# RWKV-6 attention with a mixture-of-depths layer: the scores' products in quarter tiles behind the state's products, and the accumulator banks dealt out anew

## The chip, the core and the metric

The kernel runs on one core of one Trainium2 chip. The metric is the device time of one execution in microseconds. Of the kernel before there are three runs, with a median of 201.39 us (200.97 to 201.78), and one more execution that was profiled.

## What is computed

Per batch (4), head (8) and position (768), with heads of 48 elements, a state of 48 x 48 is carried through the sequence. `w` decays it, `k` and `v` add to it, `r` reads it, and the position's own product is weighted with `u`:

```python
for t in range(S):
    cur = einsum('bhd,bhe->bhde', u * k[t], v[t])
    y[t] = einsum('bhd,bhde->bhe', r[t], state + cur)
    state = w[t][..., None] * state + einsum('bhd,bhe->bhde', k[t], v[t])
x = y, as (batch, position, 384)
scores = x @ w_gate                       # per batch and position
top = the 128 positions with the highest scores
out = x;  out[top] += sigmoid(scores[top]) * (relu(x[top] @ w1) @ w2)
```

## The kernel before

**Tiling.** The sequence of a batch is cut into 6 chunks of 128 positions, 24 chunks in all. Inside a chunk the recurrence is written as matrix products. Two heads lie side by side in each 128-partition tile, 64 partitions apiece (48 used, the rest padding), so the 8 heads are 4 pairs (`HP`), and `half(q)` names the partitions of head `q` of a pair.

**What happens to a chunk.** `inputs_t` transposes k and r on the Tensor engine (PE), `decays_t` the decays w. On the Vector engine (DVE) `scans` turns the decays into running products from the right and from the left, and `scaled` multiplies the transposed k and r with them and thereby empties their accumulator banks. `scores` multiplies K with R, 128 x 128 per head; `masked` keeps what lies before the diagonal, on DVE. `outputs_t` adds up two products in one tile `ps_yt`: the masked scores with v, and, from a batch's second chunk on, the state with R. The Scalar engine (ACT) copies that to `yt`. `rows_out` transposes it back, ACT copies it to `x`, the GpSimd engine (POOL) adds the positions' own part `vo`, and the rows are stored. `own_products`, `own_weights` (POOL), `own_values` (ACT, one small sum per head) and `own_results` make that part. `back` transposes K back (`kt`, copied by ACT), `carry_products` multiplies it with v, and `carry` adds the state and multiplies by the chunk's whole decay. There is no `back`, `carry_products` or `carry` for the last chunk of a batch, and no state in the first.

**Router.** `row_products` and `row_sums` give a score per position. `compared` ranks a chunk's scores against those of its batch: it spreads a chunk's 128 scores over a bank with a transpose (`ps_e`), DVE compares that with the chunk's own (L534) and with the earlier chunks' (L530), and ACT copies it to `every` for the later chunks. When a batch is complete, `mixture` counts the ranks (products into `ps_r`, L554), builds a selection matrix (`pick`, L571), finds the chosen rows' indices (`ps_i`), gathers the rows with an indirect DMA and transposes them (`ps_x`). `forward` is the feed-forward on them, in small pieces (`ps_h` L638, `ps_f` L650).

**Order.** All engines' programs are in the order in which `turn(i)` calls these steps: `manual_schedule` moves nothing. A turn mixes chunks: it works on chunk `i`, prepares `i+1` and `i+2`, writes out `i-1` and compares `i-2`. `fed_in_turn` puts pieces of the feed-forward of an earlier batch into two places of a turn (the first and the second feed half), and `mix` moves `mixture` on by a step in named places ("half", "mid", "end"). Semaphores between engines follow from the tiles: an instruction waits for the one that wrote what it reads, and for the last reader of a buffer that it overwrites; two engines that read one accumulator bank are also put one after the other, in the program's order.

**Accumulator banks.** [...] Before, they are dealt out in pools: `psW` one (decays, and the router's `ps_e`), `psT` two in rotation (transposes of k, of r, of K back), `psS` one tile of two banks (the scores and, after them, `ps_yt`), `psY` one (rows back), `psK` one (carry products), `psM` one (feed-forward).

**Loads.** SyncE (SP) issues the loads in `loads(i + 5)` at the end of a turn, and the stores; each of r, k, v, w has four buffers.

## Time and profile before

| | |
|---|---|
| median of three runs | 201.39 us (200.97 to 201.78) |
| profiled execution | 201.83 us, of it 200.0 us from the first to the last instruction |
| PE busy (matmuls; weight loads) | 187.9 us (153.5 us) |
| DVE, ACT, POOL busy | 159.7, 127.4, 139.0 us |
| scores (L395) | 384 instructions, 27.9 us |
| products with the state (L436) | 320 instructions, 13.1 us |
| moved by DMA | 28.81 MB |
| granted clock of PE, mean | 0.982 |

PE's busy time counts matmuls that overlap, and their ends are modelled; for the time that a group really takes, the starts of one group and the next are compared. A single-precision product is two matmul instructions in the trace, a transpose is one. "Waits" name who waited for whom; idle time of an engine that isn't the bottleneck costs nothing. In a window, a DMA share near 1 means that the core's 16 DMA engines were busy throughout. Line numbers (L395) are those of the kernel before.

### The profile page before, as it was taken

The page shows a single profiled execution, that of the slowest core. Times are in us where ns is not written, and L with a number is a line of the kernel's source. Part 1 is how long each engine was busy: PE and PEld are TensorE (multiplying, and loading weights), DVE is VectorE, ACT ScalarE, POOL GpSimd, SP SyncE. Part 2 cuts the span into 40 slices and gives each one's busy share as a digit, 9 for nine tenths or more (in the row PEclk, how much of TensorE's full clock was granted, in tenths as well). Part 3 has the DMA queues.
Part 4 walks back from the last instruction along what each step waited for, and adds up shares of the span by engine and source line. Part 5 has one row for each costly group of instructions (what it writes and reads, how often), then busy time and mean ns, then how long its engine had stood idle before and what let it go on. Part 6 is the DMA issues. An engine that isn't in the chain of part 4 may idle for free.

```text
span 200.0 us, 6426 instructions
## 1 busy us (share of the span) xinstructions
PE 187.9 (94%) x2289; PEld 153.5 (77%) x2289; DVE 159.7 (80%) x348; ACT 127.4 (64%) x653; POOL 139.0 (70%) x186
## 2 busy tenths in 40 slices
PE   7999999998899999999999999999999998899980
PEld 3578878866878888897887898897787897766940
DVE  5999999999999878989978988989978984861010
ACT  4589999998955957777557667776656576410300
POOL 8699899996878797858639798857739786121202
PEclk9999999999996999999999999999999999999996
DMA  7999999998899999999995894996744121111101
GB/s 111 163 163 158 180 187 193 219 201 154 195 201 265 182 204 220 237 195 212 188 182 123 147 212 100 141 158 139 159 67 118 47 74 44 39 43 43 39 8 44
DMA packets 105387, 28.81 MB, mean 144 GB/s; under 512 B 100482, under 2 KB 104580, under 8 KB 105348
## 3 DMA queue, kind: packets, MB, share of 16 engines
q1 hardware_dynamic: 104304, 26.65, 74.8%
q0 software_dynamic: 512, 1.57, 2.6%
q8 instruction: 20, 0.33, 0.7%
q14 instruction: 19, 0.16, 0.3%
q10 hardware_dynamic: 532, 0.10, 0.3%
HBM read 22.81 MB, written 5.51 MB: 142 GB/s over the span
## 4 chain that ended last, share of the span: by engine, by line
PE 75%; ACT 8%; DVE 7%; DMA 4%; POOL 2%; issue 2%; POOLq 0%; DVEq 0%
PE ps_h L638 11%; PE ps_s L395 11%; PE ps_f L650 11%; PE ps_yt L428 8%; PE ps_t L272 7%; PE ps_kv L483 5%; PE ps_w L272 5%; PE ps_yt L436 4%; PE ps_y L279 4%; DMA r_buf<-in_r_dram 4%; PE ps_t L279 3%; PE ps_e L528 3%; ACT rk L373 2%; DVE right_buf L292 2%; ACT yt L441 2%
## 5 line engine op out<-in xcount | busy, mean ns | idle before, releaser
L373 ACT ACTIVATE rk<-rk 128x48 f32<-128x48 f32 x192 | 44.3, 238 | 0.0
L373 ACT ACTIVATION_READ_ACCUMULATOR rk<-rk 128x1 f32 x192 | 37.3, 194 | 0.0
L453 POOL TENSOR_TENSOR x<-x,vo 128x384 f32<-128x384 f32 x22 | 22.1, 1004 | 19.0 <-ACT x L452 18.9
L303 DVE TENSOR_TENSOR_SCAN left<-ps_w,from_left 128x511 f32<-128x511 f32 x24 | 30.7, 1281 | 0.9
L403 DVE TENSOR_TENSOR sc<-ps_s,before_f 128x1024 f32<-128x1024 f32 x24 | 29.2, 1218 | 2.7 <-PE ps_s L395 2.7
L395 PE MATMUL ps_s<-R,K 48*128 48x128 f32 x384 | 27.9, 285 | 2.4 <-ACT yt L441 1.6
L292 DVE TENSOR_TENSOR_SCAN right_buf<-ps_w,from_right 128x511 f32<-128x511 f32 x24 | 29.1, 1212 | 1.0 <-PE ps_w L272 1.0
L395 PEld LDWEIGHTS ps_s<-R,K 48*128 48x128 f32 x384 | 23.3, 187 | 6.6 <-ACT yt L441 4.2
L441 ACT COPY yt<-ps_yt 128x512 f32<-128x512 f32 x24 | 14.1, 586 | 19.7 <-PE ps_yt L436 18.0
L638 PE MATMUL ps_h<-xeT,w 128*128 128x128 f32 x192 | 25.6, 280 | 0.8 <-ACT hid L643 0.8
L428 PE MATMUL ps_yt<-sc,v_buf 128*64 128x128 f32 x384 | 25.6, 275 | 0.2 <-PE ps_w L272 0.2
L638 PEld LDWEIGHTS ps_h<-xeT,w 128*128 128x128 f32 x192 | 22.9, 192 | 2.9 <-issue 1.3
L362 POOL TENSOR_TENSOR rk<-r_buf,k_buf 128x384 f32<-128x384 f32 x24 | 24.1, 1002 | 0.9 <-ACT yt L441 0.9
L365 POOL TENSOR_TENSOR rk<-rk,u_bc 128x384 f32<-128x384 f32 x24 | 24.0, 1001 | 0.9 <-DVE right_buf L292 0.4
L650 PE MATMUL ps_f<-w,hid 128*128 128x384 f32 x64 | 23.8, 500 | 0.0
L458 POOL TENSOR_TENSOR scr<-x,wg_bc 128x384 f32<-128x384 f32 x22 | 22.0, 1000 | 1.7
L428 PEld LDWEIGHTS ps_yt<-sc,v_buf 128*64 128x64 f32 x384 | 20.7, 138 | 1.0 <-PE ps_w L272 0.4
L382 POOL TENSOR_TENSOR vo<-v_buf,own 128x384 f32<-128x384 f32 (+1 forms) x24 | 17.6, 735 | 3.6 <-ACT rk L373 3.6
L350 DVE TENSOR_TENSOR R<-ps_t,left 128x512 f32<-128x512 f32 x24 | 16.4, 685 | 3.3 <-ACT own L616 1.3
L539 ACT COPY every<-ps_e 128x128 f32<-128x128 f32 x20 | 5.3, 265 | 21.0 <-DVE ahead L534 21.0
L350 DVE TENSOR_TENSOR K<-ps_t,right_buf 128x512 f32<-128x512 f32 x22 | 15.0, 680 | 3.3 <-PE ps_t L272 3.3
L272 PE MATMUL ps_w<-ident,w_buf 128*128 128x128 f32 x96 | 15.6, 288 | 0.5 <-ACT every L539 0.2
(118 smaller groups left out, 368.2 us busy)
## 6 DMA issues: line engine op xcount, KB each, us to landing
k_buf<-in_k_dram SPq DMA_DIRECT2D x24, 192.0 KB, 5.3
r_buf<-in_r_dram SPq DMA_DIRECT2D x24, 192.0 KB, 5.3
v_buf<-in_v_dram SPq DMA_DIRECT2D x24, 192.0 KB, 4.5
out_dram<-x SPq DMA_DIRECT2D x24, 192.0 KB, 3.3
w_buf<-in_w_dram SPq DMA_DIRECT2D x23, 192.0 KB, 4.8
w<-in_moe_w_dram SPq DMA_DIRECT2D x3, 512.0 KB, 5.8
w<-in_moe_w_dram SPq DMA_DIRECT2D x4, 384.0 KB, 5.1
w_buf<-in_w_dram ACTq DMA_DIRECT2D x1, 96.0 KB, 3.3
```

The lines of the kernel that those rows point to most:

```text
L272: nc.tensor.transpose(ps[:, j, :], src(j), ident)
L292: nc.vector.tensor_tensor_scan(out=flat[:, W - 2::-1], data0=wt[:, W - 1:0:-1], data1=from_right.rearrange("p j t -> p (j t)")[:, W - 2::- ...
L303: nc.vector.tensor_tensor_scan(out=left.rearrange("p j t -> p (j t)")[:, 1:W], data0=wt[:, 0:W - 1], data1=start.rearrange("p j t -> p (j ...
L350: nc.vector.tensor_mul(out, t.pop(name + "t"), t.pop(by))
L362: nc.gpsimd.tensor_mul(rk, r_bufs[n % NBUF][:, :, 0:D], k_bufs[n % NBUF][:, :, 0:D])
L365: nc.gpsimd.tensor_mul(t["rk"], t["rk"], u_bc)
L373: nc.scalar.activation(out=rk[:, h, :], in_=rk[:, h, :], func=AF.Copy, accum_out=o[:, h:h + 1])
L395: nc.tensor.matmul(ps[:, q, j, :], t["K"][rows, j, :], t["R"][rows, j, :], start=True, stop=True,)
L403: nc.vector.tensor_mul(t["sc"].rearrange("p q j t -> p (q j) t"), ps.rearrange("p q j t -> p (q j) t"), _heads(before_f, 2 * HP),)
L428: nc.tensor.matmul(ps[half(c), j % 2, j // 2, :], vt[:, 2 * j + q, :], t["sc"][:, q, j, :], start=(j < 2), stop=(old is None), skip_group_ ...
L638: nc.tensor.matmul(ps[:, q, :], w1[:, dc, (f0 + q) * L:(f0 + q + 1) * L], xeT[:, dc, :], start=(dc == 0), stop=(dc == NDC - 1),)
L650: nc.tensor.matmul(ps, hid[:, fc, :], w2[:, fc, :], start=(fc == 0), stop=(fc == NFC - 1))
```

## The change

- `scores` is done in 64 x 64 tiles: for each pair, four products of 64 columns of K instead of two of 128. It is called for chunk `i+1` directly behind `outputs_t(i)`, not for chunk `i` at the start of its turn.
- `ps_yt` gets a pool of its own, `psV` (two banks); `psS` holds the scores alone. `psY` and `psK` are gone: rows back and carry products use the two rotating banks of `psT`, and the router's and feed-forward's tiles that were there, and `ps_x`, move to `psV` or `psT`.
- k of chunk `i+2` is transposed ahead of the carry products and outputs, not at the end of the turn. Its load goes one chunk further ahead, as the last of a turn's loads.
- `compared` is split in three: the earlier chunks' comparison stays, the transpose with ACT's copy (`in_all`) comes behind `back`, and the own comparison behind `masked`.

```diff
--- before.py
+++ after.py
@@ -105,8 +105,7 @@
     psW = ctx.enter_context(tc.tile_pool(name="psW", bufs=1, space=PSUM))
     psT = ctx.enter_context(tc.tile_pool(name="psT", bufs=2, space=PSUM))
     psS = ctx.enter_context(tc.tile_pool(name="psS", bufs=1, space=PSUM))
-    psY = ctx.enter_context(tc.tile_pool(name="psY", bufs=1, space=PSUM))
-    psK = ctx.enter_context(tc.tile_pool(name="psK", bufs=1, space=PSUM))
+    psV = ctx.enter_context(tc.tile_pool(name="psV", bufs=1, space=PSUM))
     psM = ctx.enter_context(tc.tile_pool(name="psM", bufs=1, space=PSUM))
 
     chunks = [(b, ci) for b in range(B) for ci in range(NCH)]
@@ -156,14 +155,14 @@
 
     def loads(n):
         load(v_bufs, v, n - 3)
-        load(k_bufs, k, n - 1)
         load(r_bufs, r, n - 1)
         load(w_bufs, w, n)
+        load(k_bufs, k, n)
 
 
     for bufs, x, n in (
         (k_bufs, k, 0), (r_bufs, r, 0), (w_bufs, w, 1), (k_bufs, k, 1), (r_bufs, r, 1),
-        (w_bufs, w, 2),
+        (w_bufs, w, 2), (k_bufs, k, 2),
     ):
         load(bufs, x, n)
     loads(3)
@@ -388,14 +387,16 @@
             )
 
     def scores(t):
+
+
         t["ps_s"] = ps = psS.tile([L, 2, HP, L], FP32, tag="s", name="ps_s")
         for j in range(HP):
-            for q in (0, 1):
-                rows = slice(DP * q, DP * q + D)
-                nc.tensor.matmul(
-                    ps[:, q, j, :], t["K"][rows, j, :], t["R"][rows, j, :],
-                    start=True, stop=True,
-                )
+            for c in (0, 1):
+                for q in (0, 1):
+                    nc.tensor.matmul(
+                        ps[half(c), q, j, :], t["K"][half(q), j, half(c)],
+                        t["R"][half(q), j, :], start=True, stop=True,
+                    )
 
     def masked(t):
         ps = t.pop("ps_s")
@@ -420,7 +421,7 @@
         vt = v_bufs[n % NBUF]
         old = state.get(n)
 
-        ps = psS.tile([L, 2, HP, L], FP32, tag="s", name="ps_yt")
+        ps = psV.tile([L, 2, HP, L], FP32, tag="v", name="ps_yt")
 
         for j in range(HP):
             for c in (0, 1):
@@ -442,7 +443,7 @@
 
     def rows_out(t, soon=False):
         b, ci = chunks[t["n"]]
-        y = dense(psY, "y", lambda j: t["yt"][0:DE, j % 2, j // 2, :], lambda j: crossed(j, 0))
+        y = dense(psT, "t", lambda j: t["yt"][0:DE, j % 2, j // 2, :], lambda j: crossed(j, 0))
         x = t["x"] = lev.tile([L, C], FP32, tag="x", name="x", bufs=3)
         xj = x.rearrange("p (j e) -> p j e", j=HP)
         vo = t.pop("vo").rearrange("p (j q) d -> p j (q d)", q=2)
@@ -477,7 +478,7 @@
         n = t["n"]
         if chunks[n][1] == NCH - 1:
             return
-        t["kv"] = kv = psK.tile([L, HP, D], FP32, tag="kv", name="ps_kv")
+        t["kv"] = kv = psT.tile([L, HP, D], FP32, tag="t", name="ps_kv")
         for j in range(HP):
             for q in (0, 1):
                 nc.tensor.matmul(
@@ -509,7 +510,7 @@
 
     against = {}
 
-    def compared(t):
+    def others_compared(t):
 
         b, ci = chunks[t["n"]]
         if ci == 0:
@@ -521,22 +522,34 @@
                 lost_bufs[b % 2],
             )
         every, ahead, lost = against[b]
-        own = score[:, b, ci:ci + 1]
-        lo, hi = ci * L, (ci + 1) * L
-
-        ps = psW.tile([L, L], FP32, tag="w", name="ps_e")
-        nc.tensor.transpose(ps, own.to_broadcast([L, L]), ident)
         if ci > 0:
             nc.vector.tensor_scalar(
-                out=ahead[:, ci, 0:lo], in0=every[:, 0:lo], scalar1=own, scalar2=None,
+                out=ahead[:, ci, 0:ci * L], in0=every[:, 0:ci * L],
+                scalar1=score[:, b, ci:ci + 1], scalar2=None,
                 op0=ALU.is_ge, op1=ALU.add, accum_out=lost[:, ci, 0:1],
             )
+
+    def in_all(t):
+
+        b, ci = chunks[t["n"]]
+        t["e"] = ps = psW.tile([L, L], FP32, tag="w", name="ps_e")
+        nc.tensor.transpose(ps, score[:, b, ci:ci + 1].to_broadcast([L, L]), ident)
+        if ci < NCH - 1:
+            nc.scalar.copy(out=against[b][0][:, ci * L:(ci + 1) * L], in_=ps)
+
+    def own_compared(t):
+        b, ci = chunks[t["n"]]
+        ahead, lost = against[b][1:]
         nc.vector.scalar_tensor_tensor(
-            out=ahead[:, ci, lo:hi], in0=ps, scalar=own, in1=after_f,
+            out=ahead[:, ci, ci * L:(ci + 1) * L], in0=t.pop("e"),
+            scalar=score[:, b, ci:ci + 1], in1=after_f,
             op0=ALU.is_ge, op1=ALU.mult, accum_out=lost[:, ci, 1:2],
         )
-        if ci < NCH - 1:
-            nc.scalar.copy(out=every[:, lo:hi], in_=ps)
+
+    def compared(t):
+        others_compared(t)
+        in_all(t)
+        own_compared(t)
 
     def mixture(b):
 
@@ -547,8 +560,11 @@
 
 
         every, ahead, lost = against[b]
-        pool, tag = (psK, "kv") if ended else (psY, "y")
-        ps = pool.tile([L, NCH], FP32, tag=tag, name="ps_r")
+        def room(shape, name):
+            pool, tag = (psT, "t") if ended else (psV, "v")
+            return pool.tile(shape, FP32, tag=tag, name=name)
+
+        ps = room([L, NCH], "ps_r")
         for e in range(NCH):
             for c in range(e + 1):
                 nc.tensor.matmul(
@@ -573,7 +589,7 @@
                     op0=ALU.is_equal,
                 )
             yield "half"
-            ps = psK.tile([L, 2], FP32, tag="kv", name="ps_i")
+            ps = room([L, 2], "ps_i")
             for c in range(NCH):
                 nc.tensor.matmul(
                     ps, pick[:, c, :], ids[:, b, c, :], start=(c == 0), stop=(c == NCH - 1)
@@ -597,7 +613,7 @@
             yield "end"
             yield "mid"
 
-            ps = psT.tile([L, NDC, L], FP32, tag="t", name="ps_x")
+            ps = room([L, NDC, L], "ps_x")
             for dc in range(NDC):
                 nc.tensor.transpose(ps[:, dc, :], xe[:, dc * L:(dc + 1) * L], ident)
             xeT = mod.tile([L, NDC, L], FP32, name="xeT", bufs=2)
@@ -631,7 +647,7 @@
         hid = mod.tile([L, NFC, L], FP32, name="hid")
         for f0 in range(0, NFC, 4):
 
-            pool, tag = (psY, "y") if ended and f0 % 8 == 0 else (psM, "m")
+            pool, tag = (psV, "v") if ended and f0 % 8 == 0 else (psM, "m")
             ps = pool.tile([L, 4, L], FP32, tag=tag, name="ps_h")
             for q in range(4):
                 for dc in range(NDC):
@@ -644,7 +660,7 @@
                 yield q == 3
 
         load_weights(len(weights))
-        pool, tag = (psY, "y") if b == B - 1 else (psM, "m")
+        pool, tag = (psV, "v") if b == B - 1 else (psM, "m")
         ps = pool.tile([L, C], FP32, tag=tag, name="ps_f")
         for fc in range(NFC):
             nc.tensor.matmul(
@@ -716,7 +732,6 @@
         if i < 1:
             step(scaled_aside, i + 1, "K", "right")
         step(own_products, i + 1)
-        step(scores, i)
         step(own_values, i, range(FIRST))
         step(carry, i - 1, work.get(i))
         if i > 0:
@@ -728,11 +743,15 @@
         if i == N - 1:
             sums.extend(check_sums())
         if i < N:
-            step(compared, i - 2)
+            step(others_compared, i - 2)
         step(back, i)
         mix(place="half")
+        if i < N:
+            step(in_all, i - 2)
         if not soon:
             step(masked, i)
+        if i < N:
+            step(own_compared, i - 2)
         step(rows_out, i - 1, soon)
         step(row_scores_soon if soon else row_products, i - 1)
         step(own_values, i, range(FIRST, H))
@@ -750,14 +769,15 @@
         if i == -1:
             spread(u_bc.rearrange("p h d -> p (h d)"), u_row)
             step(own_weights, i + 1)
+        step(inputs_t, i + 2, "K", k_bufs)
+        if i == -2:
+            warm(1)
         step(carry_products, i)
         step(outputs_t, i)
+        step(scores, i + 1)
         fed_in_turn(PIECES - PIECES // 2, 1 if i == N - 1 else 0)
         if i == N - 1:
             step(compared, i - 1)
-        step(inputs_t, i + 2, "K", k_bufs)
-        if i == -2:
-            warm(1)
         if not soon:
             step(row_sums, i - 1)
         step(scans, i + 2)
```

## The prediction, made before the changed kernel was run

> I write "turn" for one pass of the loop over chunks, and give the groups of the Tensor engine (PE) the names of their outputs: R and K (transposes of r and k), w (of the decays), kv, yt with its two halves L428 and L436 (the latter the products with the state), scores, e (the transposed scores of the router), kt and y (the back transposes). Group times are from start to start.
>
> **What bounds the kernel now.** First the page's busy line, then the table by stretches of 10 us (columns: stretch, length, busy us and instructions of each engine, granted clock, DMA share, GB/s):
>
> ```profile
> PE 187.9 (94%) x2289; PEld 153.5 (77%) x2289; DVE 159.7 (80%) x348; ACT 127.4 (64%) x653; POOL 139.0 (70%) x186
> ```
>
> ```profile
> 30.00:40.00 10.00, 9.77 (x153) 8.17 (x150) 9.79 (x20) 9.81 (x53) 9.63 (x13) 1.00 1.02 206
> 120.00:130.00 10.00, 10.00 (x142) 8.66 (x140) 9.23 (x20) 7.49 (x39) 8.58 (x11) 1.00 0.71 121
> ```
>
> Two stages: up to about 60 us VectorE (DVE), ScalarE (ACT) and the DMA engines are all full, and a turn takes 5.84 us, which is DVE's work; from 60 to 165 us PE has no gap at all, because pieces of the feed-forward fill it. Then the late PE stream in order of time (start, busy, instruction):
>
> ```profile
> 84.09 0.65 PE L436 MATMUL ps_yt<-R,state 64*48 64x128 f32 x16
> 84.67 1.60 PE L638 MATMUL ps_h<-xeT,w 128*128 128x128 f32 x12
> 86.11 0.60 PE L272 MATMUL ps_t<-ident,k_buf 128*128 128x128 f32 x4
> 86.64 1.16 PE L395 MATMUL ps_s<-R,K 48*128 48x128 f32 x16
> 87.73 0.32 PE L528 MATMUL ps_e<-ident,score 128*128 128x128 f32 x1
> ...
> 89.35 0.60 PE L272 MATMUL ps_t<-ident,r_buf 128*128 128x128 f32 x4
> 89.78 0.60 PE L272 MATMUL ps_w<-ident,w_buf 128*128 128x128 f32 x4
> 90.31 0.67 PE L483 MATMUL ps_kv<-v_buf,kt 128*64 128x48 f32 x16
> 90.81 1.06 PE L428 MATMUL ps_yt<-sc,v_buf 128*64 128x128 f32 x16
> ```
>
> Four transposes take 0.44 before more transposes (R) and 0.53 before another tile form (w, K): leaving a form costs 0.09. Entering one costs too: after L436, 12 pieces of L638 take 1.44 against 12 x 0.112 = 1.34, so 0.10.
>
> The waits (who for whom: us in all, times, longest):
>
> ```profile
> ACT every L539 <- DVE ahead L534: 21.0, 18, 2.5
> ...
> PEld ps_s L395 <- ACT yt L441: 4.2, 8, 1.1
> ```
>
> The second is what the change removes. The first shows that ACT's copy of e waits for DVE's comparison, though both only read the bank. At 40.28 that copy starts, and w, which is next in the same single bank, starts at 40.60. So bank W is a chain: e, its two readers one after the other, then w. The ACT stream of an early turn:
>
> ```profile
> 31.82 0.59 ACT L441 COPY yt<-ps_yt 128x512 f32<-128x512 f32 x1
> ...
> 34.31 0.27 ACT L539 COPY every<-ps_e 128x128 f32<-128x128 f32 x1 [0.17 <-DVE ahead L534]
> 34.47 0.49 ACT L413 COPY kt<-ps_t 128x384 f32<-128x384 f32 x1
> ```
>
> From yt to the moment ACT is ready for e is 34.31 - 0.17 - 31.82 = 2.32: a row sum, a small copy and five own-value sums.
>
> **The Trainium skill.** "TensorEngine Tiling (Array Packing)", Key Properties: changing the tiling mode drains TensorE, tiles of one mode run independently. The trace agrees: 0.09 to leave, up to 0.10 to refill. "PSUM — Partial Sum Buffer", PSUM bank collisions: two engines must not touch one bank and quadrant at once, reads included, so a dependency is put between them; the 21.0 us above are that. "TensorE: Matmul & The Clock Gate", Architectural detail: ACT and DVE are strict FIFO; the ACT stream above, in the order of the program, agrees.
>
> **The change, part by part.** *Scores.* L436 already runs in 64x64 tiles: its starts come in rounds of four, the first after 0.146, then every 0.109. The old scores start in pairs 0.112 apart, 8 rounds. The new ones are 32 instructions, thus 8 rounds of four: 8 x 0.109 + 0.09 exit = 0.96, against 1.09. The dearest they could be is the old pace per instruction, 32 x 0.068 = 2.18; the cheapest is 0.87. I take 0.96, since L436 shows the same four tiles. Form changes per turn fall from five to three. One late turn, old: w 0.53, L436 0.58, K 0.53, scores 1.09, e 0.16 = 2.89, plus the 0.09 to refill L638. New: w 0.44, K 0.53, L436 0.49, scores 0.96, e 0.11 = 2.53, plus 0.09. Saved: **0.36** per turn where PE alone sets the pace; 0.24 in the first turn of a batch, which has no L436.
>
> *Own banks for yt.* The wait of scores for ACT's yt goes (4.2). Early it hides behind DVE, so worth nothing; at 167 us, where PE really stood still 0.71, worth at most that.
>
> *Compare split.* Now DVE's masked product (1.14 to 1.22) comes ahead of the own comparison, and ACT's copy of e ahead of that too. Nothing is added to any engine, but the chain of bank W is turned round: own-values on ACT, **kt copy**, copy of e, own comparison, then w on PE; K now stands **behind w and ahead of kv and yt**, and yt feeds ACT again. Queued behind w are K, kv, yt, L436 and scores; behind the comparison on DVE are R's scaling and both scans. Sum of this loop: e copy 0.27 + release 0.06 (an ACT yt ending at 167.57 lets scores go at 167.62) + comparison 0.35 + 0.06 + w 0.44 + K 0.53 + kv 0.50 + yt 0.99 + L436 to ACT's yt 0.72 (84.09 to 84.81) + 2.32 + kt copy 0.37 = **6.61**. Before: 0.32 + w 0.53 + 0.50 + 0.99 + 0.72 + 2.32 = 5.38, under DVE's 5.84 and so unseen.
>
> Early turns (w starts at 17.40, 23.24, 29.08, 34.92, 40.60, 46.71, 52.78, 61.10, 67.82): three of 5.84 become 6.61, +2.3; into turn 5 (last chunk, no kt) 6.24 against 5.68, +0.6; the two after it lack kv or L436, +0.1 together; turn 8 has the first ranking, +0.6 (below); turn 9, 6.61 against 6.72, -0.1. With 0.3 at the start: **+3.8**.
>
> Late turns: the same loop is hidden when feed pieces lie between. Two exceptions per batch, twice:
> - Ranking. The products for it stay behind the second feed, which now stands behind scores, and the next turn begins with kt in a rotating bank that DVE must first free.
>
> ```profile
> 100.57 0.14 DVE L560 TENSOR_REDUCE rank<-lost 128x6 f32<-128x18 f32 x1
> 101.99 0.17 DVE L561 TENSOR_TENSOR rank<-ps_r,rank 128x6 f32<-128x6 f32 x1 [1.27 <-PE ps_r L554]
> 102.19 1.07 DVE L571 TENSOR_SCALAR pick<-slots,rank 128x128 bf16<-128x128 bf16 x6
> 103.17 0.35 DVE L502 TENSOR_TENSOR mid<-ps_kv,state 128x192 f32<-128x192 f32 x1
> 103.44 0.68 DVE L350 TENSOR_TENSOR K<-ps_t,right_buf 128x512 f32<-128x512 f32 x1
> ```
>
>   From rank to mid's end is 1.5, to K's end 2.1: PE, which had scores to do here, now waits that long before kt. From w to w: K, kv, yt, L436, scores, feed and ranking products end 5.9 after w, mid 7.5, then kt, index, e, y, feed, and the index and masked product on DVE hold the comparison until 9.7; w at 10.1 to 10.6, against 8.39. I take +1.8.
> - The hidden layer's activation (L643, 0.50 of ACT) at the end of a second feed half: it is ready 0.3 after the feed, then row sum, own-values 1.8, e copy, comparison 0.74: w 7.95 after w, against 6.66: +1.3.
>
> The other late turns: -0.36 -0.24 for two per batch, and about +0.15 for those whose turn has no first feed half, or a gate's sums on ACT ahead of the copy of e (both eat the 0.36). Per batch 1.8 + 1.3 - 0.6 + 0.15 = 2.65; twice, **+5.3**.
>
> *Loads.* One more load of k ahead, behind w's on SP's queue. Early, DMA is full; k landed 1.5 before its use (41.59 and 43.09) and is now wanted some 2 earlier, but issued a turn earlier: nothing. The first v comes one issue (1.15) later, for PE at 13.2: the 0.3 above. *Tail:* scores of the last chunk no longer wait, but R's scaling before them sits behind the comparison: -0.4. Ranking, index and gather banks change names only.
>
> Sum: 3.8 + 5.3 - 0.4 = +8.7. The profiled execution took 201.83 (span 200.0), 0.44 over the median of the runs, 201.39. 201.83 + 8.7 = 210.5, less 0.44: **210.1 us**, slower. I give 210.
>
> **Rivals.**
> - *Faster, PE stays the bound (0.13).* For: PE has no gap for 100 us and loses two form changes per turn. 13 turns x 0.36 + 0.71 = 5.4: 196.0. It decides if the loop of 6.61 is in truth under the turn, that is if ACT reaches the copy of e 1.2 us sooner than its queue says. Against: every link is an order of the program or a wait in this trace.
> - *Early loop only (0.13).* The late stalls are swallowed: 201.4 + 3.8 - 12 x 0.36 - 0.4 = 200.5. Against: PE can't make up lost time in a stage that it bounds.
> - *64x64 scores at the old pace (0.06).* Row pairs not overlapping: +1.2 in some 12 late turns on top, 224. Against: L436.
> - *Main (0.68):* its own range 205 to 214.
>
> Less than 0.5% either way (200.4 to 202.4) this kernel's measurement can't tell. Faster: 0.13 + 0.05 of the second rival = 0.18; same 0.05; slower 0.77. Range 199 to 215 holds the main case and the second rival, some 0.80.
>
> **What would show it.** Right: early turns of 6.6 with ACT waiting for yt and DVE's comparison waiting for ACT's copy; w waiting for the comparison; PE gaps of about 1.5 before kt at each ranking; new scores at 0.96 straight behind L436. Wrong: early turns of 5.8, PE without gaps late, or score instructions over 0.03 us each.

## The result, and the profile after

The changed kernel takes **213.13 us** (median of four runs, 212.76 to 214.19), the kernel before 201.34 beside it (200.97 to 201.78): a ratio of **1.059**, interval 1.055 to 1.064. Its profiled execution took 212.76, with a span of 211.0, so 10.9 more than the span before (spans to the hundredth: 210.97 and 200.04). One of the four executions of e1_compare_whole and one of e2_own_sums_later below, in both the profiled one, ran at a lower granted clock (0.972 and 0.971) and is left out of their medians and ratios, and those of their turns that hold a halved clock (14 in both, 20 in the first) are not compared. In this part line numbers are those of the changed kernel: scores L396, the two halves of yt L429 and L437, ACT's copy of yt L442, of e L538, of kt L414; DVE's comparison with the earlier chunks L526, the own one L543.

The page's busy line and, from its costliest groups, the scores (instructions, then busy us and mean ns):

```profile
PE 186.7 (88%) x2673; PEld 151.8 (72%) x2673; DVE 160.3 (76%) x348; ACT 128.4 (61%) x653; POOL 139.5 (66%) x186
...
L396 PE MATMUL ps_s<-R,K 64*64 64x128 f32 x768 | 26.4, 271 | 0.0
```

The engines' work has hardly changed: PE 1.2 less, DVE 0.6 more, ACT 1.0 more. Nearly all of the 11 us is standing still. The same stretches of 10 us as before show where (stretch, length, then busy us and instructions of PE, PEld, DVE, ACT, POOL, then granted clock, DMA share, GB/s); the last row will be wanted below:

```profile
30.00:40.00 10.00, 8.24 (x136) 6.84 (x136) 9.02 (x18) 9.10 (x52) 7.92 (x10) 1.00 1.21 221
120.00:130.00 10.00, 9.67 (x134) 8.37 (x133) 7.58 (x16) 7.24 (x38) 7.67 (x9) 1.00 0.63 123
110.00:115.00 5.00, 4.91 (x31) 4.04 (x32) 3.33 (x8) 2.42 (x11) 4.57 (x6) 0.66 0.20 59
```

Early, every engine lost its full occupation: PE 9.77 to 8.24, DVE 9.79 to 9.02. When all of them have slack at once, the bound is no engine, it is a ring of waits. DMA is no bound here either, although its share rose from 1.02 to 1.21: between 25 and 58 us the trace shows no engine waiting for a load. The view of waits (us in all, times, longest) has its links:

```profile
ACT yt L442 <- PE ps_yt L437: 35.2, 20, 3.7
...
PEld ps_t L271 <- ACT kt L414: 7.3, 10, 1.1
DVE ahead L543 <- ACT every L538: 6.7, 11, 1.4
PEld ps_w L271 <- DVE ahead L543: 5.6, 9, 1.1
...
PEld ps_t L278 <- DVE mid L503: 3.6, 3, 1.7
```

ACT waits for yt; PE for ACT's copy of kt and for DVE's comparison; DVE for ACT's copy of e. (The last row, mid, belongs to the ranking below.) Both rows of before that carried its story are gone, scores waiting for ACT's yt and ACT's copy of e waiting for DVE. One turn of the ring, in order of time (start, busy, instruction, idle before it):

```profile
35.08 0.59 ACT L442 COPY yt<-ps_yt 128x512 f32<-128x512 f32 x1 [0.91 <-PE ps_yt L437]
37.30 0.47 ACT L414 COPY kt<-ps_t 128x384 f32<-128x384 f32 x1
37.66 0.27 ACT L538 COPY every<-ps_e 128x128 f32<-128x128 f32 x1
37.82 0.66 PE L271 MATMUL ps_t<-ident,r_buf 128*128 128x128 f32 x4 [0.88 <-ACT kt L414]
37.96 0.35 DVE L543 SCALAR_TENSOR_TENSOR ahead<-ps_e,score,after_f 128x128 bf16<-128x128 f32 x1
38.38 0.66 PE L271 MATMUL ps_w<-ident,w_buf 128*128 128x128 f32 x4
...
40.89 0.65 PE L437 MATMUL ps_yt<-R,state 64*48 64x128 f32 x16
41.37 1.05 PE L396 MATMUL ps_s<-R,K 64*64 64x128 f32 x32
41.61 0.59 ACT L442 COPY yt<-ps_yt 128x512 f32<-128x512 f32 x1 [0.90 <-PE ps_yt L437]
```

Start to start: yt copy to kt copy 2.22, to the copy of e 0.36, to the comparison 0.30, to w 0.42, from w to K 0.49, to kv 0.53, to yt 0.50, to L437 0.99, to the next yt copy 0.72: together 6.53, which is the turn. The scores stand straight behind L437 (0.47 after its start). Two links of the same length go from ACT back to PE here: R waits 0.88 for the copy of kt, and w, which follows 0.56 behind R, has just had its comparison finished (37.96 + 0.35 = 38.31). So two links tie here, and the ring closes through either.

Two kinds of late turn stall. A ranking turn:

```profile
107.80 0.67 PE L570 MATMUL ps_r<-minus,ahead 128*128 128x1 bf16 x21
108.50 0.16 DVE L577 TENSOR_TENSOR rank<-ps_r,rank 128x6 f32<-128x6 f32 x1 [2.18 <-PE ps_r L570]
...
110.09 0.60 PE L278 MATMUL ps_t<-turned,K 112*128 112x112 f32 x4 [1.62 <-DVE mid L503]
```

DVE waits 2.18 for ranking products that stand behind a feed half, and PE then waits 1.62 for the bank that DVE empties behind the ranking. Before, the feed half stood ahead of the ranking products too, but the scores stood behind them, so that PE had work while DVE ranked:

```profile
101.28 0.67 PE L554 MATMUL ps_r<-minus,ahead 128*128 128x1 bf16 x21
101.88 1.16 PE L395 MATMUL ps_s<-R,K 48*128 48x128 f32 x16
```

And a hidden-layer turn:

```profile
85.43 0.60 ACT L659 ACTIVATE hid<-ps_h 128x512 f32<-128x512 f32 x1 [1.12 <-PE ps_h L654]
...
86.56 0.61 DVE L526 TENSOR_SCALAR_CACHE_REDUCE ahead<-every,score 128x384 bf16<-128x384 f32 x1 [1.33 <-ACT scr L464]
86.58 0.32 PE L536 MATMUL ps_e<-ident,score 128*128 128x128 f32 x1 [1.19 <-ACT scr L464]
88.64 0.66 PE L271 MATMUL ps_w<-ident,w_buf 128*128 128x128 f32 x4 [0.23 <-DVE ahead L543]
```

The activation waits for the feed, the row sum (L464, 85.92) stands behind it on ACT, and both PE (e) and DVE (the comparison with the earlier chunks) wait for the row sum.

Where the 10.9 are, from the starts of w in the two traces, turn n being the time from the start of w in turn n-1 to that in turn n:

| turns | predicted | before | after | difference |
|---|---|---|---|---|
| up to 1 | +0.3 | 17.40 | 18.22 | +0.8 |
| 2, 3, 4 | +2.3 | 5.84, 5.84, 5.84 | 7.09, 6.53, 6.53 | +2.6 |
| 5 | +0.6 | 5.68 | 6.45 | +0.8 |
| 6, 7 | +0.1 | 6.11, 6.07 | 6.34, 6.48 | +0.6 |
| 8, 9 | +0.5 | 8.32, 6.73 | 8.14, 6.54 | -0.4 |
| 11, 17 (hidden layer) | +2.6 | 6.66, 6.66 | 8.16, 8.16 | +3.0 |
| 14, 20 (ranking) | +3.6 | 8.39, 8.39 | 11.21, 10.08 | +4.5 |
| 12, 13, 18, 19 | -1.2 | 7.25, 7.06, 7.25, 7.06 | 6.95, 6.87, 6.95, 6.87 | -1.0 |
| 10, 15, 16, 21 | +0.3 | 8.04, 6.99, 8.05, 6.99 | 8.16, 7.31, 8.58, 7.05 | +1.0 |
| behind turn 21 | -0.4 | 43.41 | 42.32 | -1.1 |

### The profile page after: what moved, and what is told of

Its sections match the earlier page's. It is cut to its first block, busy times and chain, and to the rows that moved or that the text cites. A ratio compares the mean times of both kernels' runs of the same rounds, so it can differ in the third digit from the quotient of the medians.

```text
span 211.0 us, 7151 instructions
## 1 busy us (share of the span) xinstructions
PE 186.7 (88%) x2673; PEld 151.8 (72%) x2673; DVE 160.3 (76%) x348; ACT 128.4 (61%) x653; POOL 139.5 (66%) x186
## 4 chain that ended last, share of the span: by engine, by line
PE 63%; ACT 13%; DVE 11%; SPq 6%; DMA 3%; issue 3%; POOL 0%; POOLq 0%; ACTq 0%; DVEq 0%
PE ps_f L666 11%; PE ps_yt L429 9%; PE ps_h L654 7%; PE ps_t L271 7%; PE ps_yt L437 6%; PE ps_w L271 6%; PE ps_kv L484 5%; SPq L151 5%; PE ps_s L396 5%; ACT rk L372 4%; DVE sc L404 3%; PE ps_t L278 3%; DMA v_buf<-in_v_dram 3%; ACT scr L464 3%; ACT yt L442 2%
## 5 line engine op out<-in xcount | busy, mean ns | idle before, releaser
L442 ACT COPY yt<-ps_yt 128x512 f32<-128x512 f32 x24 | 14.1, 588 | 38.9 <-PE ps_yt L437 35.2
L291 DVE TENSOR_TENSOR_SCAN right_buf<-ps_w,from_right 128x511 f32<-128x511 f32 x24 | 29.2, 1216 | 2.3 <-PE ps_w L271 1.0
L396 PE MATMUL ps_s<-R,K 64*64 64x128 f32 x768 | 26.4, 271 | 0.0
L429 PE MATMUL ps_yt<-sc,v_buf 128*64 128x128 f32 x384 | 25.6, 275 | 0.0
L666 PE MATMUL ps_f<-w,hid 128*128 128x384 f32 x64 | 24.5, 511 | 0.0
L396 PEld LDWEIGHTS ps_s<-R,K 64*64 64x64 f32 x768 | 22.2, 133 | 1.3 <-issue 1.0
L429 PEld LDWEIGHTS ps_yt<-sc,v_buf 128*64 128x64 f32 x384 | 20.6, 137 | 0.6 <-issue 0.5
L271 PE MATMUL ps_t<-ident,r_buf 128*128 128x128 f32 x96 | 15.5, 285 | 5.2 <-ACT kt L414 4.6
L271 PE MATMUL ps_w<-ident,w_buf 128*128 128x128 f32 x96 | 16.2, 294 | 3.7 <-DVE ahead L543 3.4
L271 PEld LDWEIGHTS ps_t<-ident,r_buf 128*128 128x128 f32 x96 | 11.2, 145 | 9.2 <-ACT kt L414 6.7
```

The lines of the kernel that those rows point to most:

```text
L271: nc.tensor.transpose(ps[:, j, :], src(j), ident)
L291: nc.vector.tensor_tensor_scan(out=flat[:, W - 2::-1], data0=wt[:, W - 1:0:-1], data1=from_right.rearrange("p j t -> p (j t)")[:, W - 2::- ...
L396: nc.tensor.matmul(ps[half(c), q, j, :], t["K"][half(q), j, half(c)], t["R"][half(q), j, :], start=True, stop=True,)
L429: nc.tensor.matmul(ps[half(c), j % 2, j // 2, :], vt[:, 2 * j + q, :], t["sc"][:, q, j, :], start=(j < 2), stop=(old is None), skip_group_ ...
L666: nc.tensor.matmul(ps, hid[:, fc, :], w2[:, fc, :], start=(fc == 0), stop=(fc == NFC - 1))
```

## The experiments

All but one start from the changed kernel. The ratios are to the kernel before (201.2 to 201.5 in these comparisons). Single turns are from one profile each, and a stretch of halved clock can lengthen a late one by more than 1 us (last section).

| run | median, us | ratio, interval | turn 3 | 11 | 14, 20 |
|---|---|---|---|---|---|
| changed kernel | 213.13 | 1.059 (1.055 to 1.064) | 6.53 | 8.16 | 11.21, 10.08 |
| e1_compare_whole | 211.36 | 1.047 (1.041 to 1.054) | 6.60 | 7.84 | 10.29, 10.76 |
| e2_own_sums_later | 210.27 | 1.047 (1.042 to 1.052) | 6.27 | 8.15 | 11.46, 10.09 |
| e3_k_at_end | 220.21 | 1.096 (1.090 to 1.102) | 6.64 | 7.72 | 10.10, 10.11 |
| e4_feed_behind_ranking | 208.68 | 1.038 (1.034 to 1.042) | 6.53 | 7.35 | 8.70, 8.71 |
| e5_old_tiles | 214.54 | 1.068 (1.063 to 1.074) | 6.52 | 8.37 | 11.68, 10.30 |
| e6_before_new_tiles | 200.92 | 0.998 (0.996 to 1.000) | 5.78 | 6.61 | 8.39, 8.39 |
| e7_sums_and_feed | 205.00 | 1.020 (1.015 to 1.025) | 6.27 | 6.80 | 8.71, 8.71 |
| e10_whole_sums_feed | 207.09 | 1.027 (1.022 to 1.032) | 6.32 | 6.99 | 8.39, 8.39 |
| e13_copy_behind_kt | 203.99 | 1.014 (1.010 to 1.018) | 6.32 | 6.94 | 8.39, 8.39 |
| e14_and_v_first | 204.16 | 1.013 (1.009 to 1.018) | 6.32 | 6.94 | 8.39, 8.39 |
| e16_k_behind_state | 212.42 | 1.059 (1.052 to 1.065) | 6.09 | 8.15 | 10.84, 10.10 |
| e18_k_early_old_loads | 203.45 | 1.011 (1.007 to 1.015) | 6.32 | 6.93 | 8.39, 8.39 |

### Undoing the split compare

`compared_whole` does it all at the old place: comparison with the earlier chunks, e, own comparison, and then ACT's copy of e.

```diff
         if i < N:
-            step(others_compared, i - 2)
+            step(compared_whole, i - 2)
         step(back, i)
...
-        if i < N:
-            step(in_all, i - 2)
...
-        if i < N:
-            step(own_compared, i - 2)
```

> The kernel after, with the router's comparison whole at its old place: the scores' transpose ahead of the back transposes, DVE's own comparison ahead of the masked product, ACT's copy last. All else as after. Theory (ring): the early turns are closed by two links that tie at 6.53 us: ACT's copy of e, the own comparison, w; and ACT's kt copy, the bank that r's transposes take over, R, w. Only the first is cut, and the kt copy now stands behind e's copy (0.16 more), so early turns stay at 6.5 to 6.7 and the whole at 211 to 214 us. Rival (the split alone): early turns fall to DVE's 5.8 to 6.0, the whole to 208 or less.

Measured: 211.36; the early turns keep their length, 6.60 in turn 3. Of the turns up to 7 only two fall: turn 5, which has no copy of kt (6.45 to 5.74), and turn 7, in which ACT has no copy of e, since a batch's last chunk isn't kept (6.48 to 5.84). Turn 6 got longer (6.34 to 6.83), and so turn 7 begins only 0.6 sooner than in the changed kernel. So turning the compare round was not the sole cause early: with it undone, the same ring closes over the copy of kt, which holds the bank that the next R transposes want. In the trace of this run R waits 0.65 for that copy and w follows at once. The second path that was expected as a tie is there.

### Taking the own-value sums out of the ring

```diff
-        step(own_values, i, range(FIRST))
...
-        step(own_values, i, range(FIRST, H))
+        step(own_values, i, range(H))
```

> The kernel after, with the first five own-value sums of ACT moved behind the kt, e and x copies of the turn (all eight together). No work more or less on any engine. Ring theory: both links lose the 1.15 us of the five sums, early turns fall from 6.53 to about 5.7 to 6.0 (then DVE's work closes them), the two turns behind a hidden-layer activation fall from 8.16 by about 1.1, the ranking turns stay: 206 to 208 us. Rival (PE's form changes or the 64x64 scores are what costs): nothing on PE changes, 213 us. Rival (ACT is simply full): the same work, 213 us.

Measured: 210.27; turns 2 to 5 at 6.26, 6.27, 6.32 and 6.45. The direction is right, but 5.7 to 6.0 was expected: with ACT out of the way, DVE closes the next ring. In turns 3 and 4 PE's transposes of K back wait 0.28 and 0.24 for DVE's scaling of K, and in turn 4 w waits 0.20 for the comparison; in turn 5 the latter is longest. Around w's start in turn 5, in order of time:

```profile
42.91 0.34 DVE L543 SCALAR_TENSOR_TENSOR ahead<-ps_e,score,after_f 128x128 bf16<-128x128 f32 x1
...
43.32 0.66 PE L271 MATMUL ps_w<-ident,w_buf 128*128 128x128 f32 x4 [0.91 <-DVE ahead L543]
```

The own comparison stands behind DVE's masked product now, w behind the comparison, and DVE's scan (L291, 44.01) behind w. The hidden-layer turn is unchanged, 8.15: the sums were not what held it, which the row sum's waits above already say.

### Putting K back to the end of the turn

```diff
-        step(inputs_t, i + 2, "K", k_bufs)
-        if i == -2:
-            warm(1)
         step(carry_products, i)
         step(outputs_t, i)
...
         if i == N - 1:
             step(compared, i - 1)
+        step(inputs_t, i + 2, "K", k_bufs)
+        if i == -2:
+            warm(1)
```

> The kernel after, with k's transposes back at the end of the turn, behind the second feed half. Ring theory: the ring loses K's 0.53 us, early turns fall from 6.53 to about 6.0, the turns behind a hidden-layer activation by about 0.5, ranking turns stay: 208 to 210 us. Rival (k's place only matters for the loads): 213 us.

A miss, and the largest: 220.21, where 208 to 210 was expected. The waits of this run:

```profile
DVE K L349 <- PE ps_t L271: 20.1, 17, 2.2
PEld ps_w L271 <- DVE ahead L543: 14.3, 20, 1.5
...
PEld ps_t L278 <- DVE K L349: 7.8, 15, 0.6
```

At the end of the turn K stands behind scores (0.98) and, late, a feed half. DVE waits for it with the scaling of K, up to 2.2; the masked product and the own comparison queue behind that scaling, and w behind the comparison. And since y now shares the two rotating banks with K, y waits for the scaling too. Before, y had a bank of its own and K stood ahead of the scores. So "K forward" is no ornament of the change: with the shared banks and the later scores, K has to stand ahead of the scores, and undoing one part alone breaks another. (Which of the two, the banks or the scores, costs how much was not separated.)

### Moving K by a smaller step

The same step in another place, up to turn 6: behind the products with the state, ahead of the scores.

```diff
-        step(inputs_t, i + 2, "K", k_bufs)
+        if i > 6:
+            step(inputs_t, i + 2, "K", k_bufs)
+        step(carry_products, i)
+        step(outputs_t, i)
+        if i <= 6:
+            step(inputs_t, i + 2, "K", k_bufs)
         if i == -2:
             warm(1)
-        step(carry_products, i)
-        step(outputs_t, i)
```

> The kernel after, with one step of the order moved up to turn 6: the transposes of k stand behind the products with the state (ahead of the scores), not behind w and ahead of kv and yt. Theory: both links of the early ring (copy of e to w, and copy of kt to R) run through K, 0.53, and yt; with K out of it the early turns 1 to 5 fall from 6.53 to 6.0 to 6.15 and later turns stay: 1.5 to 2.5 less in all, 210.6 to 211.6. It also tells what went wrong with e3_k_at_end, where K stood at the end of the turn: here its scaling and the two rotating banks should keep their order. Rival (as in e3: the banks need K ahead of kv): early turns 6.5 or more, 213 or more.

Turns 3, 4 and 5 take 6.09, 6.12 and 6.22 instead of 6.53, 6.53 and 6.45: K, a group of 0.53, gives 0.44, 0.41 and 0.23. What stays is w's wait for the comparison, 0.17 of its weight load in turn 4, and 0.79 in turn 5. The link is shown, and turns 3 and 4 give most of its term. The sum gains less, 212.42, whose interval overlaps the changed kernel's, because turn 1 got longer (6.91 against 6.40; the first v is waited for 1.47) and turns 6 and 7 don't move.

### Moving the second feed half behind the ranking

```diff
-        fed_in_turn(PIECES - PIECES // 2, 1 if i == N - 1 else 0)
         if i == N - 1:
+            fed_in_turn(PIECES - PIECES // 2, 1)
             step(compared, i - 1)
...
         mix(place="end")
+        if i != N - 1:
+            fed_in_turn(PIECES - PIECES // 2, 0)
```

> The kernel after, with the second feed half of a turn issued behind the ranking products and the scans, not ahead of them. Theory: the ranking products stand 1.4 us earlier in PE's stream, so DVE ranks and picks while PE works on the feed; PE's gap of 1.6 us ahead of kt in the two late ranking turns falls to about 0.3; early turns stay at 6.53: 210 to 211 us. Rival (the gap comes from the bank that kt waits for, whatever PE does before): 213 us.

Measured: 208.68, better than expected, 4.4 less than the changed kernel. The ranking turn again:

```profile
105.52 0.68 PE L570 MATMUL ps_r<-minus,ahead 128*128 128x1 bf16 x21
...
107.82 0.60 PE L278 MATMUL ps_t<-turned,K 112*128 112x112 f32 x4 [0.22 <-DVE mid L503]
```

The ranking products now stand ahead of the feed, which runs while DVE ranks: PE's wait for mid falls from 1.62 to 0.22, and turn 20 from 10.08 to 8.71. The hidden-layer turn falls too, 8.16 to 7.35: the row sum no longer stands behind the activation. The early turns don't move. This settles that the late loss came from the order of scores, feed half and ranking products: with the scores gone from behind the ranking products, PE needed other work there, and the feed half is such work.

### The tile form by itself, at either place

Two runs split the form of the scores from the rest of the change. First the changed kernel with the old 64x128 products:

```diff
-            for c in (0, 1):
-                for q in (0, 1):
-                    nc.tensor.matmul(
-                        ps[half(c), q, j, :], t["K"][half(q), j, half(c)],
-                        t["R"][half(q), j, :], start=True, stop=True,
-                    )
+            for q in (0, 1):
+                nc.tensor.matmul(
+                    ps[:, q, j, :], t["K"][half(q), j, :], t["R"][half(q), j, :],
+                    start=True, stop=True,
+                )
```

> The kernel after, with the scores' products in their old form (two per pair of heads, 16 in all, 64x128) at the new place and in the new bank. Theory of the prediction: behind the products with the state the scores now change form (about 0.09 to leave, up to 0.10 to enter) and take 1.09 to 1.16 instead of 0.98, so about 0.3 more per turn, but only in turns where nothing else makes the Tensor engine wait: early turns stay 6.53 (the scores are not in the ring of bank W), the ranking and hidden-layer turns hide most of it, some 8 to 10 late turns show it: +2.4 to +3.0, about 215.5 to 216. Rival (the new form itself costs time, since it has twice as many instructions): 212 or less. Second rival (the scores lie under other work everywhere): within 0.5 of 213.1.

And the kernel before with the new products at the old place (the same edit, the other way round):

> The kernel before, with the scores in 32 products of 64x64 at their old place (behind K, ahead of the router's e), and nothing else changed. Theory: the rounds of four are what makes the scores cheaper, 0.98 against 1.09 to 1.16 (0.1 to 0.18 less), and being next to the products with the state saves the changes of form on top, which stays five here; early turns stay at 5.84, 13 late turns gain 0.1 to 0.18: 199.0 to 200.1. Rival (all of the saving lies in the neighbour of the same form): 201.0 to 201.5. Second rival (64x64 is dearer next to full tiles): over 202.

Busy time hardly tells the forms apart (27.9 and 26.5 us for all groups of the two runs); the clearest reading is two turns that PE alone paces, 12 and 13:

| turns 12, 13 | kernel before (old place) | changed kernel (new place) |
|---|---|---|
| 64x128 products | 7.25, 7.06 | 7.17, 6.92 |
| 64x64 products | 7.19, 7.00 | 6.95, 6.87 |

The form gives 0.06 at the old place, 0.22 and 0.05 at the new one; the new place, with all else that the change moves, gives 0.08 and 0.14 with the old form. Both together are 0.30 and 0.19. In all, the new form is worth 0.5 at the old place (200.92 against 201.46 in the same comparison, an interval of 0.9963 to 0.9997 that just excludes no change) and 1.4 at the new one (214.54 against 213.13, whose intervals overlap a little). At the new place 2.4 to 3.0 was expected, so the saving is about half of that. That the 64x64 form is dearer is excluded at the old place and unlikely at the new one.

One more thing is in turn 3 of e6_before_new_tiles: 5.78 against 5.84. So even before, a turn was DVE's work and a little of PE's: cheaper scores shortened it.

### Both repairs at once

> The kernel after with two edits at once: all own-value sums of the Scalar engine behind its late call, and the second half of the feed behind scans and ranking products. If the two losses are separate (an early ring and late gaps before the rank), their gains add: 213.1 less 2.1 less 4.45, about 206.5, early turns 6.3, ranking turns 8.7, hidden-layer turns 7.35. If what one gains the other takes (the Tensor engine alone sets the sum late), no better than 208.7. Theory that the early own-value sums are also what holds the router's e in the hidden-layer turns: these fall to 7.0 or less.

Measured: 205.00. The gains of the two edits alone, 2.9 and 4.5, add up to 205.8, which lies inside the interval of this run (1.015 to 1.025 of 201.46 is 204.5 to 206.5): the two losses are separate. The hidden-layer turn falls to 6.80, which neither did alone, so with the activation out of the way the own-value sums were next there. From turn 8 to turn 21 this kernel takes 95.7, the kernel before 95.5: **what is left of the loss, 2.6 of span, is 3.4 up to turn 8, less 1.0 at the end.**

### Trying to get the early turns back

To this the compare whole was added, as in the first experiment.

> The kernel after with the compare whole again at its old place, all own-value sums behind the late call, and the second half of the feed behind scans and ranking products. Theory: early there are two links of almost the same length (ring of bank W, and the small copy of kt that holds the bank which the next transposes want); with both taken away the early turns fall to the Vector engine's own work, 5.8 to 6.0 instead of 6.53, 3 less over turns 1 to 7; late turns as in the run with the feed moved. About 203, range 201.5 to 205. Rival (one more limit at 6.3, the comparison that w waits for, or the row sums that arrive late): 206 to 208, early turns 6.2 or more.

The rival was right: 207.09, turns 3 and 4 at 6.33 and 6.34. The end is 1.6 longer than in e7_sums_and_feed: ACT's copy of e waits 2.09 for the comparison in front of the hidden layer's activation, and PE 1.65 for that. So ACT's copy (`e_copied`) was moved behind that of kt, and, with `compared`, ahead of the own comparison in turn 22:

```diff
-        if i < N:
-            step(compared_whole, i - 2)
+        if i < N - 1:
+            step(compared_own_first, i - 2)
+        if i == N - 1:
+            step(compared, i - 2)
         step(back, i)
+        if i < N - 1:
+            step(e_copied, i - 2)
```

> As the run e10_whole_sums_feed (compare whole ahead of the back transposes, all own-value sums late, second half of the feed behind scans and ranking), but the Scalar engine copies e behind the copy of kt, not ahead of it, and in turn 22 (two from the end) it copies e ahead of the own comparison, as the kernel after does. Theory: in e10 the early turn of 6.34 is a ring of the Vector engine's own comparison, the copy of e that waits for it (0.74), the copy of kt behind that, the R transposes that wait for kt's bank (0.6), R's scaling (0.35 idle ahead of it). Without the wait the copy of kt comes 0.3 sooner and the Vector engine has no idle time: early turns 5.75 to 5.9. In the last turns the copy of e waited 2.09 in e10 and held up the hidden layer's activation, which then held the Tensor engine 1.65; without that the stretch behind turn 21 is 42.4 instead of 44.0. In sum 4 less than e10's 207.1: 202 to 204. Rival (another limit at 6.3 early, such as the loads of k): early turns 6.2 or more, 205 to 206.

Half right: 203.99; the end falls by 1.1 to 42.9, but turn 3 stays at 6.32. On top of that, the first loads were put in another order:

```diff
-        (w_bufs, w, 2), (k_bufs, k, 2),
+        (w_bufs, w, 2),
...
-    loads(3)
+    load(v_bufs, v, 0)
+    load(k_bufs, k, 2)
+    load(r_bufs, r, 2)
+    load(w_bufs, w, 3)
+    load(k_bufs, k, 3)
```

> As e13_copy_behind_kt, with the loads at the start in another order: the first v ahead of the third k, as before the change. Theory of the prediction: the late first v delays the first turns by 0.3; the runs so far have turn 1 at 6.2 to 6.4 from w to w against 5.64 before, so up to 0.7 may lie there: 0.3 to 0.7 less than e13. Rival (turn 1 is slow for the same ring as the later ones): no difference to e13 beyond 0.1.

No difference (204.16): turn 1 got 0.55 longer and turn 2 0.62 shorter, and turn 3 begins at the same time to 0.01. PE no longer waits for v in turns 0 and 1, but 1.42 for the third k in turn 0. Which of the two loads comes first doesn't matter. Last, K late up to turn 6, with the loads in the order of before:

> As e13_copy_behind_kt, with K behind the products with the state up to turn 6 and the loads in the order of the kernel before (one load of k less ahead, the first v's earlier). Theory: in e13 the early turn of 6.32 is the ring yt copy, row sum, e, back transposes of K, copy of kt, R, w, K, kv, yt; with K (0.53) out of it the Vector engine's own work of 5.7 to 5.8 is the bound again. And e13 lost 1.6 up to turn 2, where kv waited for v, which stands behind one more load of k. Both gone, turn 7 begins near 53, as before the change, instead of 56.05: 3 less than e13's 204.0, so 201 (200 to 202), beside 201.4 before. Rival (loads of k land too late in this order): turn 7 at 55 or later, 203 or more.

The rival's figures came true, but not its reason: 203.45, turn 7 at 55.40, and turns 3 and 4 still 6.33 and 6.33; from 13 us to the end of turn 7 the trace shows no engine waiting for a load. Two views of this run show what bounds these turns. The first is one turn, from one copy of kt to the next, as a stretch (columns as above):

```profile
23.18:29.50 6.32, 5.88 (x104) 4.73 (x103) 5.87 (x12) 5.61 (x30) 5.72 (x8) 1.00 1.03 182
```

The second is its end in order of time (L558 is e, L414 the copy of kt):

```profile
28.76 0.33 PE L558 MATMUL ps_e<-ident,score 128*128 128x128 f32 x1 [0.26 <-ACT scr L464]
...
29.50 0.48 ACT L414 COPY kt<-ps_t 128x384 f32<-128x384 f32 x1 [0.72 <-PE ps_t L278]
```

ACT works 5.61 and waits 0.72: together the turn. This ring is read from the trace; no run opened it. With the own-value sums moved to the late call, nothing is left on ACT between the row sum and the copy of kt, and that copy waits while PE does e and then kt, both behind the row sum. The five sums that lengthened the first ring had covered just this wait: the repair of one ring made another. No version of the changed kernel beats the kernel before; the best, e18_k_early_old_loads, takes back 9.7 of the 11.8. A version with K late, the compare whole and the sums in their early place was not run.

## Why the prediction was right, and where its steps were off

Predicted were 210 (199 to 215), slower; measured 213.13, slower and in the main case's own range.

- **The ring of bank W: right, term by term.** 6.61 was predicted for an early turn, 6.53 measured, with the links in the order given. K's term is shown by e16_k_behind_state, ACT's by e2_own_sums_later, as far as the next ring let it. What it missed is that a second link of the same length, the copy of kt to R's bank, closes the same ring, so that undoing the compare alone gives nothing in turns 2 to 4.
- **The turn before as DVE's work alone: nearly.** Cheaper scores took 0.06 off the 5.84, as e6_before_new_tiles shows; it moved no number of the prediction.
- **The start: the term was too small.** +0.3 was given, for a first v one issue later. Turn 2 ends 2.07 late, of which the ring accounts for 0.69, as in turns 3 and 4, so the start cost about 1.4. The trace has kv waiting 0.43 for v in turn 0 and 0.55 in turn 1. "One more load of k ahead: nothing" was the step that failed: from 5 to 15 us DMA moves 163 GB/s in both kernels, so a load more ahead puts back those behind it; the first two v are issued at 8.38 and 13.27 in place of 7.14 and 12.04. In e14_and_v_first a v in front only passed the delay to k. With the loads in the order of before, e18_k_early_old_loads ends turn 2 0.66 sooner than e13_copy_behind_kt (24.20 against 24.86) and keeps that lead to turn 7; K's place changed in the same run, so the share of the loads alone isn't measured.
- **Turns 6 and 7: +0.1 became +0.6.** The prediction said that lacking kv or L436 shortens their ring. It left out that w waits there for the comparison behind DVE's masked product (in the changed kernel 0.91 in turn 5, 0.18 in turn 6 and 0.45 in turn 7), a chain that has none of the links that they lack. For turn 7 e1_compare_whole agrees: with the comparison ahead of the masked product it takes 5.84 in place of 6.48. For turn 6, which got longer there, this is read from the trace only.
- **Ranking turns: right in mechanism and size** for turn 20 (+1.69 against +1.8; PE's wait 1.62 against 1.5). Turn 14 cost +2.82: right behind its gap PE's granted clock is 0.66 over 5 us (the row above). The kernel before has such a stretch across turns 8 and 9 (0.69 from 60 to 65 us), which fits that these two came out 0.9 under their prediction. That the two stretches roughly cancel in the sum is luck.
- **Hidden-layer turns: +1.50 against +1.3, by another last link.** The prediction went from the row sum through ACT's own-values and copy of e to the comparison. In the trace that copy is ready at 87.90, and DVE's other arm ends later: row sum, comparison with the earlier chunks, masked product, behind which the own comparison starts at 88.24, and w at 88.64. e2, which takes the own-values out, left 8.15; e4, which takes the activation from ahead of the row sum, gave 7.35.
- **Scores: 0.98 against 0.96 predicted**, but 0.30 and 0.19 saved in a turn that PE paces, where 0.36 and 0.24 were given. Of the 0.30 the form by itself is 0.06 to 0.22, of the 0.19 it is 0.05 to 0.06; the rest came with the new place. From the scores' start to the next group it is 1.40 in turn 4 (start 41.37), because e, next on PE, waits 0.35 for ACT's row sum. In turn 16 (start 124.28) it is 1.40 too, and 1.42 in e4_feed_behind_ranking; there the trace names no one whom PE waited for (0.20 and 0.17 of its weight loads' idle time are put down to "issue"), so the cause of this 0.42 is open. It is about what turn 16 lost beyond its +0.15.
- **Own banks for yt: as predicted.** The wait of scores for ACT's yt is gone and nothing came of it but, at most, part of the -1.1 at the end. No run gave yt, rows back and carry products their old banks again, so this rests on the traces.

The sum was 2.2 of span short: 0.9 up to turn 4 (1.1 more at the start, 0.2 less in the ring's three turns), 0.5 in turns 6 and 7, 0.4 in the hidden-layer turns, 0.7 in turns 10, 15, 16 and 21 and 0.2 each in turn 5 and in the turns with a gain, less 0.7 that the end gave back more than predicted. In the medians it is 3.1: the profiled execution of before is 0.5 over its median, that of after 0.4 under its own.

The Trainium skill, "TensorEngine Tiling (Array Packing)", Key Properties, has a change of tiling mode drain the engine: the runs agree, since the same 32 products cost 0.98 right behind products of their own form (L437) and 1.035 between two groups of full tiles (e6_before_new_tiles).

## What to carry to other kernels

When a bank or buffer is shared by two steps, write down the ring that it closes, with the start-to-start time of each link, for the old and the new order, and compare its sum with the busiest engine's work per turn: here 5.38 under 5.84 was free, and a ring predicted at 6.61 and measured at 6.53 cost 0.69 in each of turns 3 and 4. Before a work group is moved, look at what its old place covered: the scores had kept PE at work while DVE ranked, without them PE stood 1.62 us ahead of kt, and the feed half put in their place took 1.4 us off turn 20. And when two rings tie, a repair of one shows nothing (turn 3 took 6.60 after it, 6.53 before), and a repair that moves work may uncover the wait that the work had hidden; look for "busy plus wait = turn" on each engine before the next try.

## What was not expected of the hardware

Ten of the fourteen traces have, inside the work, a stretch in which PE's granted clock is 0.50: before from about 59.6 to 63.0, after from about 110.9 to 114.3. Worked out from windows of 2 us, it is 3.4 us in both, thus 1.7 of PE's time. In the changed kernel it follows the gap of 1.62 ahead of kt in turn 14. Six kernels have such a gap there, of 1.46 to 1.63, and in five of them the stretch begins 0.3 to 1.6 us behind its end; none of the eight others has a stretch in that turn. But e3_k_at_end has the gap and no stretch in its work at all, most gaps of turn 20 are followed by none, and in the kernel before PE was busy 11.70 of the 12 us from 54 to 66. The Trainium skill, "TensorE: Matmul & The Clock Gate", Part 1, has the clock halved after at least one idle window of about 3.4 us. The length agrees; but the gaps ahead of these stretches are shorter than that, and the kernel before shows hardly any, so what starts a stretch stays open. A single turn's difference of 1 to 2 us between two profiles should be read beside the clock first.
